# A pad of 384 bytes in the constants of an attention and expert kernel

## The chip, the cores and the metric

The kernel runs on one core of a Trainium2 chip. The metric is the time of one execution on the device in microseconds (us). The engines are TensorE (PE in the profile, with PEld for its weight loads), VectorE (DVE), ScalarE (ACT), GpSimd (POOL) and SyncE (SP); transfers run on 16 DMA engines.

## The reference

Linear attention with decay, and behind it a feed-forward pair of products with a SiLU. For 4 batches, 8 heads, 768 positions and head size 64, in blocks of 64 positions:

```
intra = (qb @ kb^T * Dmask) @ vb            # Dmask[i, j] = lam^(i-j) for i >= j, else 0
inter = (qb * lam^(pos+1)) @ kv_state
out   = intra + inter
kv_state = lam^64 * kv_state + (kb * lam^(63-pos))^T @ vb
```

The outputs of all heads, side by side, are x of 3072 tokens by 512. Then `h = x @ w_in` (512 by 2048), `g = h * sigmoid(h)`, `y = g @ w_out` (2048 by 512). All inputs and the output are float32; the kernel's products run in bfloat16.

## The kernel before

**Work.** The kernel takes the sequence in 12 pairs of 128-position units (two blocks of 128 to a pair, `U = 128`), 24 units in all. For each pair, `load_pair` (L358) issues the loads of k, q and v into staging tiles `raw` (4,096 bytes a partition; for pair 0 in two halves, tiles of 2,048 bytes). A DRAM run of one load is 512 bytes long: two positions of one head. `prepare` (L458) turns them into bfloat16: `cast` (L467) gives `kq`, `scale_v` (L470) gives `vd`, v times its decay. k and q are then turned head-dimension-first into `kqT`: for the first four pairs by PE (L510) and a copy, from the fifth on by a DMA transpose from `kq` to `kqT` (L525). Scores, states and outputs of the attention are small matmuls on quarters of the array (L558, L565, L591, L602 and, for the first pairs, L692, L772, L803, L811, L822); VectorE masks the scores into `st` with `tri` (L346 is the helper `mult`, L337 and L341 the helper `copy`), carries the state over `y` and `xf`, and writes the attention's output, scaled, into `xt`.

**Weights.** `load_w` (L377) loads w_in and w_out in 16 halves of 512 KB into the same staging tiles (`raw_w`; a DRAM run is 2,048 bytes), and each half is cast in two pieces by GpSimd, ScalarE or VectorE into `w_in_bf` and `w_out_bf` (L332 and L333, 16,384 bytes a partition each), which stay for the whole run.

**Products.** `product1` (L846) multiplies `w_in_bf` by `xt` (L858) and ScalarE takes the SiLU into `g` (L874); `product2` (L882) multiplies `g` by `w_out_bf` (L893), a copy brings the bank to `osb`, and ScalarE's queue stores it (L909). The last unit is stored in two halves of 128 KB.

**Order.** Nothing is scheduled at run time. `Planner` (L38) takes every piece of work with an estimated cost, and writes out one order for each engine (L932); the launch then issues the work in that order (L955 to L964). Loads stand in SyncE's queue in the order of `sequence` (L399), and the DMA transposes stand in the same queue; the stores have ScalarE's. In the first 19 us small matmuls on the tile `ones` (L930) are put into PE's planned gaps.

**Memory.** All constants come from one pool, `const`, and all working tiles from another, `sb`; a tile is placed behind the one allocated before it, at a multiple of 32 bytes. The order of the constants is `lam_sb`, `ones`, `ident`, `spot`, `row_i`, `tri`, `xe_all`, `xs_all`, `pose`, `row`, `log_all`, `log_lam`, `lam_v`, `lam_xe`, `lam_be`, `w_in_bf`, `w_out_bf`; behind them come the working tiles, in the order of their first use. `ones` is made at L291:

```
    ones = const.tile([128, 512], BF16, name="ones")
    nc.vector.memset(ones, 1.0)
    halves = [slice(0, 64), slice(64, 128)]
    ident = const.tile([128, 128], BF16, name="ident")
```

Of the kernel before, what the change touches and what calls it, by code (L numbers as in the profile page):

```python
# [8 lines left out]
F32 = mybir.dt.float32  # L9
# [222 lines left out]
def kernel(  # L232
# [30 lines left out]
    const = ctx.enter_context(tc.tile_pool(name="const", bufs=1))  # L263
# [27 lines left out]
    ones = const.tile([128, 512], BF16, name="ones")  # L291
    nc.vector.memset(ones, 1.0)  # L292
    halves = [slice(0, 64), slice(64, 128)]
    ident = const.tile([128, 128], BF16, name="ident")
    nc.gpsimd.memset(ident, 0.0)
    nc.gpsimd.affine_select(
# [698 lines left out]
```

## Time and profile before

| what | value |
|---|---|
| median of 3 runs | 215.47 us (215.08 to 215.98) |
| the profiled execution's own time | 215.7 us |
| its span, first to last instruction | 213.7 us |
| granted PE clock, mean | 0.998 |
| PE busy | 204.7 us, 2364 matmuls |
| ScalarE, VectorE, GpSimd busy | 115.5, 109.8, 22.6 us |
| moved by DMA | 38.09 MB in 62247 packets, mean 178 GB/s |
| of that SyncE's queue (q1) | 31.46 MB in 58480 packets |
| of that ScalarE's queue (q10) | 6.30 MB in 3744 packets |

The page shows one profiled execution. Its rows give busy time with its share of the span and, behind an x, the count of instructions; rows in slices cut the span into 40 equal parts, a digit being the busy share in tenths. The chain that ended last is followed back from the last instruction to what released each step. In the timeline a line is start, duration, engine, source line, operation, output <- input, shape and count, and in brackets the idle time before it with what ended it. A row of a DMA queue gives packets, MB and the packets' time as a share of 16 engines' time in the window asked for; packets overlap, so that share can pass 100%. A row of a stage gives its bounds and length, the busy time of PE, PEld, DVE, ACT and POOL with their counts, the granted clock, the DMA engines' share and GB/s.

### The profile page before, as it was taken

To read this page: it belongs to the slowest core of one execution; us is meant where nothing else is said; L and a number is where in the kernel's file an instruction comes from. 1 tells how busy PE (TensorE), PEld (TensorE's weight loads), DVE (VectorE), ACT (ScalarE), POOL (GpSimd) and SP (SyncE) were. 2 spreads that over 40 slices of the span, in tenths; PEclk is the share of its full clock that TensorE was granted. 3 is DMA by queue.
4 is the path that set the end of the run, shared out by engine and by line. 5 is a ranking of instruction groups with operands and counts; after the bars stand their busy time and mean duration, and the time that the engine had idled before them with its cause. 6 is when DMAs were issued, how large, how long until landed. Compare 5 with 4: busy or idle time off the path is not lost.

```text
span 213.7 us, 5445 instructions
## 1 busy us (share of the span) xinstructions
PE 204.7 (96%) x2364; PEld 122.5 (57%) x2364; DVE 109.8 (51%) x188; ACT 115.5 (54%) x169; POOL 22.6 (11%) x39
## 2 busy tenths in 40 slices
PE   7788989999899999999999999999999999999994
PEld 2666777776666557676765545454444444444453
DVE  3788849688523849688988696557011100111000
ACT  3665867758571686537596773514444444444121
POOL 4005421222100400001120010300000000000000
PEclk9999999999999999999999999999999999999999
DMA  4999999999999999899999251011011001110212
GB/s 119 294 324 363 351 326 278 377 287 377 213 326 290 296 284 319 156 248 295 241 277 222 66 101 49 5 52 49 0 52 49 13 36 49 49 52 0 98 49 98
DMA packets 62247, 38.09 MB, mean 178 GB/s; under 512 B 18064, under 2 KB 55184, under 8 KB 62224
## 3 DMA queue, kind: packets, MB, share of 16 engines
q1 hardware_dynamic: 58480, 31.46, 58.2%
q10 hardware_dynamic: 3744, 6.30, 8.0%
q8 instruction: 18, 0.29, 0.6%
q14 instruction: 5, 0.04, 0.1%
HBM read 27.27 MB, written 6.29 MB: 157 GB/s over the span
## 4 chain that ended last, share of the span: by engine, by line
PE 75%; DMA 12%; SPq 8%; DVE 2%; ACT 1%; issue 1%; POOL 1%
PE banks L893 37%; PE banks L858 31%; DMA raw_w<-in_moe_w_out_dram 7%; DMA raw<-in_q_dram 5%; SPq L364 4%; SPq L383 4%; PE banks L602 2%; PE banks L558 2%; PE banks L565 1%; DVE st L346 1%; PE banks L591 1%; POOL w_out_bf L343 1%; ACT g L874 0%; DVE kq L341 0%; PE banks L510 0%
## 5 line engine op out<-in xcount | busy, mean ns | idle before, releaser
L858 PE MATMUL banks<-xt,w_in_bf 128*128 128x256 bf16 (+1 forms) x576 | 116.1, 308 | 0.9 <-DVE st L346 0.7
L893 PE MATMUL banks<-w_out_bf,g 128*128 128x512 bf16 (+1 forms) x400 | 113.3, 371 | 0.7 <-POOL w_out_bf L343 0.7
L874 ACT ACTIVATE g<-banks 128x512 bf16<-128x512 f32 x96 | 70.1, 742 | 63.3 <-PE banks L858 57.1
L858 PEld LDWEIGHTS <-w_in_bf 128*128 128x128 bf16 x576 | 55.4, 98 | 31.6 <-POOL w_in_bf L343 1.2
L893 PEld LDWEIGHTS <-g 128*128 128x128 bf16 x400 | 38.5, 98 | 40.4 <-issue 1.2
L341 DVE COPY osb<-banks 128x512 f32<-128x512 f32 x13 | 9.0, 692 | 57.0 <-PE banks L893 51.7
L346 DVE TENSOR_TENSOR st<-banks,tri 128x512 bf16<-128x512 f32 (+1 forms) x42 | 29.6, 757 | 3.4 <-PE banks L602 2.4
L339 ACT ACTIVATE kq<-raw 64x512 bf16<-64x512 f32 (+2 forms) x32 | 24.0, 780 | 4.1 <-DMA raw<-in_k_dram 1.7
L346 DVE TENSOR_TENSOR xt<-banks,lam_xe 128x512 bf16<-128x512 f32 x24 | 15.7, 686 | 14.4 <-PE banks L558 13.6
L346 POOL TENSOR_TENSOR xf<-y,lam_be 128x256 f32<-128x256 f32 (+1 forms) x13 | 11.0, 848 | 89.3 <-DVE y L720 89.3
L341 DVE CAST kq<-raw 64x512 bf16<-64x512 f32 (+3 forms) x26 | 13.4, 534 | 5.6 <-DMA raw<-in_k_dram 2.7
L346 DVE TENSOR_TENSOR vd<-raw,lam_v 128x1024 bf16<-128x1024 f32 (+1 forms) x13 | 15.0, 1152 | 1.8 <-DMA raw<-in_v_dram 1.8
L339 ACT ACTIVATE osb<-banks 128x512 f32<-128x512 f32 (+1 forms) x12 | 6.7, 561 | 16.5 <-PE banks L893 16.5
L930 PE MATMUL banks<-ones 128*128 128x128 bf16 (+1 forms) x88 | 9.7, 259 | 1.5 <-DVE ones L292 1.5
L346 DVE TENSOR_TENSOR xs_all<-y,lam_be 64x256 bf16<-64x256 f32 (+2 forms) x21 | 10.4, 497 | 0.4
L602 PE MATMUL banks<-kqT 64*64 64x128 bf16 x288 | 9.5, 217 | 0.0
L930 PEld LDWEIGHTS <-ones 128*128 128x128 bf16 x88 | 5.9, 102 | 3.9 <-issue 2.1
L602 PEld LDWEIGHTS <-kqT 64*64 64x64 bf16 x288 | 7.4, 107 | 0.0
L510 PE MATMUL banks<-ident,kq 128*128 128x128 bf16 x64 | 5.3, 220 | 1.9 <-DVE kq L341 1.4
L720 DVE TENSOR_TENSOR y<-banks,xf 128x256 f32<-128x256 f32 (+1 forms) x17 | 6.7, 398 | 0.6 <-POOL xf L346 0.5
L591 PE MATMUL banks<-vd,kq 64*64 64x64 bf16 x240 | 6.9, 194 | 0.0
L339 ACT ACTIVATE kqT<-banks 128x512 bf16<-128x512 bf16 (+1 forms) x6 | 4.9, 810 | 2.7 <-PE banks L510 2.7
(50 smaller groups left out, 79.0 us busy)
## 6 DMA issues: line engine op xcount, KB each, us to landing
out_dram<-osb ACTq DMA_DIRECT2D x23, 256.0 KB, 2.0
raw<-in_k_dram SPq DMA_DIRECT2D x11, 512.0 KB, 6.6
raw<-in_q_dram SPq DMA_DIRECT2D x11, 512.0 KB, 7.1
raw<-in_v_dram SPq DMA_DIRECT2D x11, 512.0 KB, 7.5
raw_w<-in_moe_w_in_dram SPq DMA_DIRECT2D x8, 512.0 KB, 8.8
raw_w<-in_moe_w_out_dram SPq DMA_DIRECT2D x8, 512.0 KB, 7.0
raw<-in_k_dram SPq DMA_DIRECT2D x2, 256.0 KB, 5.2
raw<-in_q_dram SPq DMA_DIRECT2D x2, 256.0 KB, 5.6
```

The lines of the kernel that those rows point to most:

```text
L339: nc.scalar.activation(o, i, AF.Copy)
L341: nc.vector.tensor_copy(o, i)
L346: (nc.vector if e == "DVE" else nc.gpsimd).tensor_tensor(o, a, b, op=AL.mult)
L364: nc.sync.dma_start(out=tile_of(bufs[i, g], [128, 2 * len(ms), 128], F32, "raw"), in_=src[i][heads(ms)].rearrange("h (p r) d -> p h (r d)" ...
L383: nc.sync.dma_start(out=tile_of(b, [128, 2, 512], F32, "raw_w"), in_=w_in_r[:, 2 * h:2 * h + 2, cs] if what == "i" else w_out_r[:, 4 * j + ...
L591: mm = nc.tensor.matmul(psum_of(db)[d, 256 * c + 64 * k:256 * c + 64 * k + 64], lhsT=kq_of()[halves[c], 0, r, 2 * k + (h ^ c if n in CROSS ...
L602: nc.tensor.matmul(t[c, k % 2, r, :], lhsT=t_of()[halves[row], 0, r, k, c], rhs=t_of()[halves[row], 1, :, k, c], start=(k % 2 == 0 and r = ...
L720: nc.vector.tensor_tensor(tile_of(src, [128, NP, 64], F32, "y")[:, sl], d_of(), old[0].tile[:, sl], op=AL.add)
L858: nc.tensor.matmul(t[:, j, :], lhsT=w_in_bf[:, ko, 128 * m:128 * m + 128], rhs=xt[gi].tile[:, ko, :], start=(ko == 0), stop=(ko == KI - 1))
L874: nc.scalar.activation(t, psum_of(bank).rearrange("p (jc r a) -> p jc r a", r=2, a=64), AF.Silu)
L893: nc.tensor.matmul(psum_of(bank)[:, :w], lhsT=g.tile[:, j, 128 * gp:128 * gp + 128], rhs=w_out_bf[:, ko, cs], start=(ko == 0), stop=(ko == ...
L930: nc.tensor.matmul((t if b.pool == "bank" else t[:, 0])[:, 0:w], lhsT=ones[:, 0:128], rhs=ones[:, 0:w], start=True, stop=True)
```

## The change

One tile of 96 float32 elements, 384 bytes in each of the 128 partitions, is allocated from `const` between `ones` and `ident`. Nothing writes or reads it. Every tile that is allocated later lies 384 bytes higher.

```
     halves = [slice(0, 64), slice(64, 128)]
+
+    const.tile([128, 96], F32, name="pad")
     ident = const.tile([128, 128], BF16, name="ident")
```

## The prediction

> **What bounds the kernel now.** I read the page first: the shares by engine, the forty slices, then the chain that ended last. Two stretches show: in the first quarter the DMA engines are full and TensorE (PE) has gaps; behind it PE is the bound.
>
> ```profile
> span 213.7 us, 5445 instructions
> PE 204.7 (96%) x2364; PEld 122.5 (57%) x2364; DVE 109.8 (51%) x188; ACT 115.5 (54%) x169; POOL 22.6 (11%) x39
> ...
> DMA  4999999999999999899999251011011001110212
> ...
> PE 75%; DMA 12%; SPq 8%; DVE 2%; ACT 1%; issue 1%; POOL 1%
> ```
>
> A slice is 213.7 / 40 = 5.34 us. The DMA row is full to slice 21, about 112 us. Of the chain 75% is PE; the 12% DMA and 8% SPq (SyncE's queue, held up while it issues loads) are what a change to transfers can touch. Next I asked where in time that 20% lies: the chain in order of time, from 18 us to 60 us.
>
> ```profile
> 18.44 9.64 DMA raw<-in_q_dram
> ...
> 28.11 0.70 DVE kq L341
> ...
> 34.19 6.50 DMA raw_w<-in_moe_w_out_dram
> ...
> 40.74 0.88 POOL w_out_bf L343
> ...
> 46.83 8.54 DMA raw_w<-in_moe_w_out_dram
> ...
> 55.42 0.62 POOL w_out_bf L343
> ```
>
> All of it lies before 55.42 us. The last transfer on the chain is a half of w_out that lands at 46.83 + 8.54 = 55.37 us; GpSimd casts it, and PE goes on. Then I asked for busy time by stage (busy us of each engine, the granted clock, the DMA share, GB/s).
>
> ```profile
> 18.00:28.00 10.00, 9.06 (x140) 6.94 (x129) 7.25 (x14) 7.63 (x12) 4.89 (x8) 1.00 1.10 345
> 28.00:42.00 14.00, 13.25 (x191) 10.35 (x189) 10.37 (x14) 9.96 (x15) 2.72 (x4) 1.00 1.07 327
> 42.00:56.00 14.00, 13.55 (x182) 9.30 (x180) 10.60 (x20) 9.31 (x14) 3.31 (x5) 1.00 1.09 325
> 56.00:112.00 56.00, 55.92 (x789) 37.49 (x789) 38.36 (x65) 34.92 (x53) 5.70 (x6) 1.00 1.14 266
> 112.00:150.00 38.00, 37.84 (x513) 19.70 (x511) 26.59 (x47) 20.16 (x30) 2.49 (x3) 1.00 0.35 78
> ```
>
> PE lacks 0.94 us in 18 to 28, then 0.75 and 0.45 us, but 0.08 us in the 56 us behind that, although the DMA engines are as full there (share 1.14). A busy PE need not run at its peak, so one row of the whole chain checks it:
>
> ```profile
> 72.63 6.04 PE banks L893 x28
> ```
>
> 28 matmuls of 512 columns in 6.04 us are one each 0.216 us, 2.37 columns a nanosecond, at a granted clock of 1.00; the 0.376 to 0.39 us that a single one lasts is latency that overlaps. From 56 us PE streams without a break, and an earlier transfer is worth nothing there. So the change is worth what it takes out of PE's gaps before 56 us. These are PE's gaps after 18 us with what ended them, from the timeline, and beside the first one the two instructions that ended just before it:
>
> ```profile
> 19.56 1.37 PE L858 MATMUL banks<-xt,w_in_bf 128*128 128x256 bf16 x11 [0.74 <-DVE st L346]
> 28.86 0.62 PE L510 MATMUL banks<-ident,kq 128*128 128x128 bf16 x8 [0.59 <-DVE kq L341]
> 41.66 0.81 PE L893 MATMUL banks<-w_out_bf,g 128*128 128x512 bf16 x3 [0.16 <-POOL w_out_bf L343]
> 56.08 1.02 PE L893 MATMUL banks<-w_out_bf,g 128*128 128x512 bf16 x4 [0.54 <-POOL w_out_bf L343]
> ```
>
> ```profile
> 18.86 0.63 ACT L339 ACTIVATE w_in_bf<-raw_w 128x512 bf16<-128x512 f32 x1 [0.72 <-DMA raw_w<-in_moe_w_in_dram]
> 18.32 1.21 DVE L346 TENSOR_TENSOR st<-banks,tri 128x1024 bf16<-128x1024 f32 x1
> ```
>
> The first gap is put down to the mask on VectorE (DVE), which ended at 18.32 + 1.21 = 19.53. But the matmul reads xt and w_in_bf, not st, and a cast of w_in_bf that had waited for its transfer ended at 18.86 + 0.63 = 19.49: I take it for a DMA gap too. So all four gaps hang on transfers: 0.74 + 0.59 + 0.16 + 0.54 = 2.03 us.
>
> **The change part by part.** It adds no instruction, no wait and no DMA, and the planner's costs are not touched, so each engine's order should stay the same. It moves every tile allocated behind `ones` by 384 bytes. In the program before, `w_in_bf` begins at byte 27,776 of a partition, which is 54 x 512 + 128. `w_in_bf`, `w_out_bf` and all tiles behind them have sizes that are multiples of 1,024 bytes, so all of them begin 128 bytes past a multiple of 512, and after the change at one. Since 384 is 3 x 128, no address changes its place within a line of 128 bytes. Only what works in pieces of 256 or 512 bytes can tell the difference: I cost the engines' own reads and writes at nothing (PE above streams at full rate from the shifted tiles already), and look at the DMAs.
>
> What does a DMA packet cost? The first view is a stretch in which only q, k, v travel (pieces of 512 bytes), the second one with weights alone (2,048 bytes), the third the start, whose queue q10 carries the little load of lam (pieces of 32 bytes), the last everything up to 56 us.
>
> ```profile
> DMA packets 1160, 0.58 MB, mean 292 GB/s; under 512 B 18, under 2 KB 1160, under 8 KB 1160
> ```
>
> ```profile
> DMA packets 407, 0.78 MB, mean 391 GB/s; under 512 B 25, under 2 KB 25, under 8 KB 407
> ```
>
> ```profile
> q10 hardware_dynamic: 137, 0.00, 1.5%
> ```
>
> ```profile
> DMA packets 21981, 17.29 MB, mean 309 GB/s; under 512 B 729, under 2 KB 17877, under 8 KB 21973
> ```
>
> The first two stretches are 2 us long. Sixteen engines for 2,000 ns carry 1160 - 18 = 1142 pieces of 512 bytes: 28.0 ns each. In the second, 382 pieces of 2,048 bytes: 83.8 ns, less some 0.5 ns for the 25 small ones, 83.3 ns. The difference, 55.3 ns for 1,536 bytes, is 0.036 ns a byte, so a 512-byte piece is 18.4 ns of bytes and 9.6 ns fixed. A third of the time of a q, k or v load is a fixed price per packet; 391 GB/s in the second stretch against 292 in the first shows that the memory does not set the pace of the small ones. The lam load's packets cost 1.5% x 16 x 4,000 ns / 137 = 7.0 ns with 1.2 ns of bytes, so 5.8 ns fixed. These are too short to cross a 256-byte line, all others cross one or more and start off it. So 9.6 - 5.8 = 3.8 ns of a packet could be the price of the broken start.
>
> The trace has no load to an address on a 512-byte line, so the saving is bounded, not read: at most 9.6 ns a packet (all that is fixed), and nothing, or below nothing, at the other end. I take 3.8 ns, by the lam row, the nearest that lacks the broken start. Up to 56 us there are 21981 - 729 = 21252 packets, 1328 on each engine, so each nanosecond saved lands the last half of w_out 1.33 us earlier; 3.8 ns give 5.0 us. Does the saving come in time for each gap? The packets up to 18, 28 and 41 us:
>
> ```profile
> DMA packets 7227, 4.71 MB, mean 262 GB/s; under 512 B 329, under 2 KB 6473, under 8 KB 7226
> ```
>
> ```profile
> DMA packets 10985, 8.16 MB, mean 292 GB/s; under 512 B 430, under 2 KB 9211, under 8 KB 10983
> ```
>
> ```profile
> DMA packets 15793, 12.39 MB, mean 302 GB/s; under 512 B 558, under 2 KB 12847, under 8 KB 15789
> ```
>
> Less the small ones these are 6898, 10555 and 15235; by 16 and 3.8 ns, 1.6, 2.5 and 3.6 us. PE needs 0.74, 1.33 and 1.49 us there, and 2.03 at the end: covered each time, and a saving of 2.03 / 1.33 = 1.53 ns a packet already closes the last gap. So the size of the saving hardly matters, if there is one: **the gaps cap the gain at 2.03 us**. Next late is PE itself. The cap may leak both ways: VectorE is busy 7.25 of 10 us around the first gap and its mask ends 0.03 us before PE starts, so 0.74 may not come back whole; and the PE work before 18 us may begin a little earlier, since VectorE's scaling of v waits for a landing there:
>
> ```profile
> 16.15 1.44 DVE L346 TENSOR_TENSOR vd<-raw,lam_v 128x1024 bf16<-128x1024 f32 x1 [0.38 <-DMA raw<-in_v_dram]
> ```
>
> That is 0.38 us more at best. Behind 56 us, and in the stores, I cost the change at nothing: PE hides loads, transposes and stores, and only the last store is bare, with eight pieces of 1,024 bytes to an engine, 0.03 us at 3.8 ns.
>
> Sum: 215.7 us (the profiled execution, span 213.7 and 2.0 around it) - 2.03 = 213.7. Its time lies 0.23 above the median of 215.47, so against that: **213.4 us**.
>
> A rule of the Trainium skill bears on this. "DMA: Bandwidth & Descriptors", section "How a descriptor splits into AXI transactions", says that a transaction must start on a 256-byte line, and that a descriptor which does not fetches the bytes below its start as well and pays their beats. Here that would be 128 bytes, four beats; at the page's clock of 850 MHz some 4.7 ns, an estimate from it. It would give the same capped sum as my 3.8 ns. But it is worded for reads, and speaks against the change so far: the loads read device memory and only write the tiles. By the wording, only stores and transposes gain, which is the first rival's time.
>
> **The rivals.** *The loads don't care* (or the allocator drops a tile that nobody uses, and nothing moves). The fixed 9.6 ns may be the price of any large packet, and the 5.8 of a small one. For it: the stores, which read the tiles, cost about what the loads do,
>
> ```profile
> q10 hardware_dynamic: 1152, 2.10, 10.1%
> ```
>
> (150 to 205 us: 10.1% x 16 x 55,000 / 1152 = 77 ns on the mean of 2,048-byte pieces and one small in nine, some 86 ns for a large one), though reading and writing need not be hurt alike. Then only stores and transposes could gain, behind PE: 0.03 us at the last store, 215.4 us.
>
> *The loads become dearer.* One mechanism: pieces that all begin on a 512-byte line fall on the same part of the memory where they were spread before, and each packet waits one step more. For the price I take the same 3.8 ns, with the other sign: the last half of w_out lands 5.0 us later, PE has nothing to put in its place, 215.5 + 5.0 = 220.5 us. There is no cap on this side. It decides from 0.8 ns a packet (0.8 x 1.33 = 1.08 us, half a per cent). For it speaks nothing in the trace but that it cannot exclude it; against it, that it is the packets with broken starts whose fixed price is the larger.
>
> **How the numbers follow.** About 0.5%, 1.1 us, is what a measurement of this kernel can tell from no change. Forecast 213.4: 0.52, of which 0.03 falls within half a per cent (a saving under 0.8 ns). Loads don't care, 215.4: 0.34, with 0.02 on either side for what else shifts. Dearer, up to 220.5: 0.14. So faster 0.49 + 0.02 = 0.51, same 0.03 + 0.30 = 0.33, slower 0.14 + 0.02 = 0.16. The forecast's own range is 212.8 (the cap, 0.38 us before 18 us and the spread of the runs, 0.3) to 214.4; to hold 8 in 10 it must reach the first rival's 215.4 and its spread: 212.8 to 216.0. Left out are the dearer packets.
>
> **What would show it.** Right: the two 2 us stretches carry more than 1142 and 382 pieces; the casts of w_out wait less; the gap before PE at 56 us is gone; PE from there on takes as long as before. Wrong: the same 28.0 and 83.3 ns a packet (then the loads don't care), or the packets get cheaper and the gaps stay, held by VectorE's mask or a cast. Fewer packets in such a stretch, and a longer gap before the last cast of w_out, are the dearer loads.

## The result, and the profile after

The changed kernel takes 212.66 us (median of 6 runs, 212.10 to 214.22) against 215.98 us (median of 6, 215.08 to 216.35) for the kernel before: a ratio of 0.986, 95% interval 0.982 to 0.990. The profiled execution took 212.1 us, its span is 210.1 us, 3.6 us shorter than before; it is the fastest of the six, and between the medians lie 3.3 us. The order of the instructions on every engine is the same in both, so the two profiles can be laid on each other line by line; line numbers are higher by 2.

The page of the changed kernel: span, busy time, the slices of the DMA engines, SyncE's queue, and the chain that ended last.

```profile
span 210.1 us, 5445 instructions
...
PE 203.6 (97%) x2364; PEld 122.4 (58%) x2364; DVE 109.4 (52%) x188; ACT 115.1 (55%) x169; POOL 23.6 (11%) x39
...
DMA  4999999999999997999974141011011101110212
...
q1 hardware_dynamic: 58480, 31.46, 52.7%
...
PE 93%; DMA 2%; POOL 1%; DVE 1%; issue 0%; SPq 0%; ACT 0%; POOLq 0%; DVEq 0%
```

The same 58480 packets move the same 31.46 MB, but take 52.7% of 210.1 us where they took 58.2% of 213.7: 124.4 and 110.7 us of packet time on each of 16 engines. The chain has turned: PE from 75% to 93%, DMA from 12% to 2%, and SyncE's queue from 8% to nothing. Now the stages (the same columns as before: busy us of PE, PEld, DVE, ACT, POOL, granted clock, DMA share, GB/s).

```profile
18.00:28.00 10.00, 9.91 (x144) 7.96 (x143) 7.25 (x13) 8.43 (x13) 4.76 (x7) 1.00 1.10 373
28.00:42.00 14.00, 14.00 (x246) 10.60 (x244) 10.97 (x16) 10.05 (x15) 2.46 (x4) 1.00 1.07 340
42.00:56.00 14.00, 14.00 (x136) 10.24 (x135) 10.97 (x22) 9.65 (x14) 2.92 (x4) 1.00 1.12 328
56.00:112.00 56.00, 56.00 (x785) 36.86 (x783) 39.19 (x66) 34.79 (x52) 5.67 (x5) 1.00 1.03 273
```

PE's gaps of 0.94, 0.75 and 0.45 us are 0.09, 0 and 0. The timeline of PE shows how far each step has come forward: these are the matmuls that began at 18.20, 28.86 and 56.08 us before.

```profile
17.21 2.04 PE L860 MATMUL banks<-xt,w_in_bf 128*128 128x256 bf16 x15 [0.43 <-POOL w_in_bf L345]
...
26.43 0.62 PE L512 MATMUL banks<-ident,kq 128*128 128x128 bf16 x8
...
52.52 1.03 PE L895 MATMUL banks<-w_out_bf,g 128*128 128x512 bf16 x4
```

0.99 us at the first product, 2.43 at the second mark, 3.56 at the third, and 3.6 at the end of the span. Everything is won before 56 us, and nothing is lost or won behind it. Between the first two marks lie 0.69 us at the next product (19.56 before, 17.88 now, in the middle of the first row) and 0.74 at the transposes; between the last two 0.32 at the products of w_out that began at 41.66, 0.13 at one that began at 52.46, and 0.70.

Last the packets, in the 2 us of the changed kernel that the prediction used for the 512-byte pieces, and in 2 us that hold weights alone:

```profile
DMA packets 1363, 0.70 MB, mean 352 GB/s; under 512 B 21, under 2 KB 1361, under 8 KB 1362
```

```profile
DMA packets 414, 0.80 MB, mean 400 GB/s; under 512 B 23, under 2 KB 23, under 8 KB 414
```

1340 pieces of 512 bytes where there were 1142, so at most 23.9 ns each for 28.0; and 391 pieces of 2,048 bytes where there were 382. The short pieces have become 4 ns cheaper; the long ones have hardly changed.

### The profile page after: what moved, and what is told of

Its sections match the earlier page's. It is cut to its first block, busy times and chain, and to the rows that moved or that the text cites. A ratio compares the mean times of both kernels' runs of the same rounds, so it can differ in the third digit from the quotient of the medians.

```text
span 210.1 us, 5445 instructions
## 1 busy us (share of the span) xinstructions
PE 203.6 (97%) x2364; PEld 122.4 (58%) x2364; DVE 109.4 (52%) x188; ACT 115.1 (55%) x169; POOL 23.6 (11%) x39
## 3 DMA queue, kind: packets, MB, share of 16 engines
q1 hardware_dynamic: 58480, 31.46, 52.7%
## 4 chain that ended last, share of the span: by engine, by line
PE 93%; DMA 2%; POOL 1%; DVE 1%; issue 0%; SPq 0%; ACT 0%; POOLq 0%; DVEq 0%
PE banks L860 40%; PE banks L895 40%; PE banks L560 2%; DMA raw<-in_v_dram 2%; PE banks L604 2%; PE banks L512 2%; PE banks L567 1%; PE banks L932 1%; PE banks L593 1%; PE banks L824 1%; POOL xf L348 1%; PE banks L774 1%; POOL w_in_bf L345 1%; SPq L366 0%; PE banks L805 0%
## 5 line engine op out<-in xcount | busy, mean ns | idle before, releaser
L860 PEld LDWEIGHTS <-w_in_bf 128*128 128x128 bf16 x576 | 55.4, 98 | 31.3 <-POOL w_in_bf L345 0.9
L348 POOL TENSOR_TENSOR xf<-y,lam_be 128x256 f32<-128x256 f32 (+1 forms) x13 | 12.0, 926 | 89.4 <-DVE y L722 89.4
L348 DVE TENSOR_TENSOR vd<-raw,lam_v 128x1024 bf16<-128x1024 f32 (+1 forms) x13 | 14.7, 1134 | 1.3 <-DMA raw<-in_v_dram 1.3
L593 PEld LDWEIGHTS <-kq 64*64 64x64 bf16 x240 | 5.7, 109 | 0.9 <-issue 0.7
```

Of the source, the lines that this page charges most:

```text
L348: (nc.vector if e == "DVE" else nc.gpsimd).tensor_tensor(o, a, b, op=AL.mult)
L593: mm = nc.tensor.matmul(psum_of(db)[d, 256 * c + 64 * k:256 * c + 64 * k + 64], lhsT=kq_of()[halves[c], 0, r, 2 * k + (h ^ c if n in CROSS ...
L860: nc.tensor.matmul(t[:, j, :], lhsT=w_in_bf[:, ko, 128 * m:128 * m + 128], rhs=xt[gi].tile[:, ko, :], start=(ko == 0), stop=(ko == KI - 1))
```

## The experiments

My theory after the result: a short piece that begins off a 256-byte line in the staging tile is dearer by some 4 ns, and that alone makes the gain. Rivals: the line is one of 512 bytes; the price goes by the bytes below the start, as the rule of the Trainium skill has it ("DMA: Bandwidth & Descriptors", section "How a descriptor splits into AXI transactions"); or the loads have no part in it, and the other tiles gain. Ratios are to the kernel before, run on the same chip. Code is shown in part and against the changed kernel; the remarks behind # are not in the kernels.

**Loads alone.** A kernel that only loads, 4 MB at a time, into one tile at various distances from a 512-byte line, and then stores. All products, casts and masks are left out.

```
PHASES = [(512, 0), (512, 128), (2048, 0), (2048, 128), (512, 256), (512, 32), (512, 64), (512, 384), (2048, 256),
          (512, 0), (512, 128)]
...
        for i in range(8):
            o = off // 4 + 1024 * i
            to = buf[:, o:o + 1024]
```

> All products, casts and masks are left out; the outputs are rows of the loaded tile. SyncE alone loads 11 times 4 MB into one tile, with nothing beside it: pieces of 512 bytes that begin 0, 128, 256, 32, 64, 384, 0 and 128 bytes past a 512-byte line, and pieces of 2,048 bytes at 0, 128 and 256; then 12 stores of 256 KB read the tile at 128 and 12 at 0. Before: 28.0 ns a 512-byte piece and engine, 83.3 ns a 2,048-byte one. Lines of 256 bytes: 512-byte pieces take some 24 ns at 0 and 256 and some 28 ns at 32, 64, 128 and 384. Lines of 512 bytes: 24 ns at 0 alone, 28 at 256 too. Bytes below the start (the rule's beats): 24 at 0 and 256, about 25 at 32, 26 at 64, 28 at 128 and 384. Contention with the engines' reads, not the pieces themselves: the same at every offset. For the 2,048-byte pieces, a price per packet would give some 79 ns at 0 and 256 against 83 at 128.

Packets in 2 us of this kernel, once a phase runs evenly: 512-byte pieces at 0, at 128, at 256 and at 32 bytes past the line.

```profile
DMA packets 1382, 0.69 MB, mean 347 GB/s; under 512 B 26, under 2 KB 1382, under 8 KB 1382
```

```profile
DMA packets 1150, 0.58 MB, mean 290 GB/s; under 512 B 16, under 2 KB 1150, under 8 KB 1150
```

```profile
DMA packets 1371, 0.69 MB, mean 347 GB/s; under 512 B 16, under 2 KB 1371, under 8 KB 1371
```

```profile
DMA packets 1145, 0.58 MB, mean 289 GB/s; under 512 B 16, under 2 KB 1145, under 8 KB 1145
```

Without the small ones, 32,000 ns hold 1356, 1134, 1355 and 1129 pieces: 23.6 ns on a line of 256 bytes, 28.2 to 28.3 off it. The phases at 64 and 384 bytes (1134 and 1135 pieces) and the repeats of 0 and 128 say the same. So it is the line of 256 bytes, not of 512; and 32 bytes off cost what 128 do. That last point is not the rule's: a beat for each 32 bytes below the start would have made the piece at 32 bytes some 25 ns, an estimate by the clock of that page of the Trainium skill. The engines' reads have no part, since no engine read the tile in these windows.

**Other sizes, and stores.** The same kernel with pieces of 256 to 2,048 bytes, each on the line and 128 bytes off it, and the stores apart from the loads.

```
PHASES = [(512, 0), (512, 128), (256, 0), (256, 128), (1024, 0), (1024, 128), (1536, 0), (1536, 128), (2048, 0), (2048, 128)]
```

> All products, casts and masks are left out; the outputs are rows of the loaded tile. As loads_alone, with other piece sizes, each first on a 512-byte line and then 128 bytes off: 512, 256 (half the bytes), 1,024, 1,536 (three quarters), 2,048 from w_out; then 12 stores off the line and 12 on it, apart from the loads. In loads_alone a 512-byte piece took 28.2 ns off the line and 23.6 on it. A fixed price of a broken start, 4.7 ns a piece at every size: 256 some 14 against 19 ns, 1,024 some 42 against 47, 1,536 some 61 against 66, 2,048 some 80 against 85. A price that only shows where a piece is short, hidden behind something else in long ones: the difference is there at 256 and 512 and shrinks to nothing by 2,048, as the two phases of loads_alone look. Stores, which read the tile: 4.7 ns dearer off the line if the rule's beats hold, the same if not.

Four of its 2 us views: 1,024 bytes on the line and off it, 1,536 on it and off it.

```profile
DMA packets 770, 0.77 MB, mean 385 GB/s; under 512 B 18, under 2 KB 770, under 8 KB 770
```

```profile
DMA packets 697, 0.70 MB, mean 349 GB/s; under 512 B 16, under 2 KB 697, under 8 KB 697
```

```profile
DMA packets 540, 0.79 MB, mean 394 GB/s; under 512 B 31, under 2 KB 539, under 8 KB 539
```

```profile
DMA packets 546, 0.79 MB, mean 395 GB/s; under 512 B 32, under 2 KB 546, under 8 KB 546
```

| piece | on the line, ns | off it, ns |
|---|---|---|
| 256 bytes | 14.8 | 18.8 |
| 512 | 23.6 | 28.2 |
| 1,024 | 42.6 | 47.0 |
| 1,536 | 63.0 | 62.3 |
| 2,048 (loads_alone) | 81.0 | 81.4 |

Each is 32,000 ns by the pieces in the best even 2 us of its phase. A short piece pays 4.0 to 4.6 ns for a start off the line, whatever its length up to 1,024 bytes; from 1,536 bytes on a load pays nothing that can be seen. These long phases do not run evenly (windows of 2 us from 88 to 62 ns at 1,536), so a small price could hide there; 4.6 ns would show in the best windows, which differ by less than 1 ns. The stores read the tile in pieces of 2,048 bytes: first off the line, then on it.

```profile
DMA packets 415, 0.76 MB, mean 381 GB/s; under 512 B 43, under 2 KB 43, under 8 KB 415
```

```profile
DMA packets 445, 0.81 MB, mean 404 GB/s; under 512 B 51, under 2 KB 51, under 8 KB 445
```

372 against 394 pieces: some 86 and 81 ns, so on the reading side a long piece does pay about 5 ns. In the attention kernel the stores are hidden and this is worth nothing. Why a long write is spared stays open.

**Pad of 128 bytes.** All tiles behind the constants at 256 past a multiple of 512.

```
-    const.tile([128, 96], F32, name="pad")
+    const.tile([128, 32], F32, name="pad")
```

> Pad of 128 bytes in place of 384: weights and all tiles behind them begin 256 bytes past a multiple of 512. If lines of 256 bytes decide, the time is that of the changed kernel, ratio 0.986 to before, some 212.7 us. If lines of 512 bytes decide, each 512-byte piece still crosses one, and it is that of before, 1.00, or between.

212.42 us, ratio 0.986 (0.984 to 0.989): the whole gain. A line of 256 bytes is enough.

**Pad of 416 bytes.** All tiles 32 bytes past a multiple of 512.

```
-    const.tile([128, 96], F32, name="pad")
+    const.tile([128, 104], F32, name="pad")
```

> Pad of 416 bytes: weights and all tiles behind them begin 32 bytes past a multiple of 512, so every 512-byte piece crosses a line of 256 and one of 512, but lies only 32 bytes off. If crossing decides, ratio 1.00 to before, 215 to 216 us. If the bytes below the start decide (one beat in place of four), a quarter of the price stays: ratio 0.988 to 0.99, some 213 us, near the changed kernel.

216.01 us, ratio 1.002 (1.000 to 1.004): the whole gain is lost. That a piece begins off the line decides, not how far off.

**Staging tiles alone on the line, and its reverse.** The staging tiles get a pool of their own; a small tile in front of one pool puts the other working tiles, or in the reverse the staging tiles, 128 bytes off.

```
+    stage = ctx.enter_context(tc.tile_pool(name="stage", bufs=1))
+    sb.tile([128, 32], F32, tag="off", name="off")        # stage_only
+    stage.tile([128, 32], F32, tag="off", name="off")     # stage_off, with
+    sb.tile([128, 96], F32, tag="on", name="on")
+            where = stage if b.pool in ("raw", "rawh") else sb
```

> The staging tiles raw lie in a pool of their own on multiples of 512 bytes, weights too; all other working tiles (kq, kqT, vd, st, xt, xf, y, g, osb) lie 128 bytes off, as before. If the loads into the staging tiles are what gains, the time is that of the changed kernel, ratio 0.986, some 212.7 us. If it is the engines' reads and writes of the other tiles, or the DMA transposes and stores, it is that of before, 1.00.

> The reverse of stage_only: the staging tiles raw begin 128 bytes off the line, weights and all other working tiles on it. If the loads into the staging tiles are the whole of it, ratio 1.00 to before, 215 to 216 us; if the other tiles have a share, below that by the share.

Staging alone on the line: 212.62 us, ratio 0.987 (0.984 to 0.990). Staging alone off it: 215.65 us, 1.000 (0.998 to 1.002). The loads of q, k, v and the weights into these tiles are the whole of the gain; no run here moved the two kinds apart, and that the weights' loads have little part in it follows from the prices by length above. The weights' place, the transposes, the stores and what the engines read and write have none that can be measured. In the reverse, PE's gaps are back where they were, here the one at 28.86 us and the one behind it:

```profile
28.86 0.62 PE L516 MATMUL banks<-ident,kq 128*128 128x128 bf16 x8 [0.59 <-DVE kq L347]
41.53 0.81 PE L899 MATMUL banks<-w_out_bf,g 128*128 128x512 bf16 x3 [0.24 <-POOL w_out_bf L349]
```

**The first pair off the line.** Everything on the line but the six staging tiles of pair 0.

```
+    head = ctx.enter_context(tc.tile_pool(name="head", bufs=1))
+    head.tile([128, 32], F32, tag="off", name="off")
+    sb.tile([128, 96], F32, tag="on", name="on")
+            where = head if b.pool == "rawh" else sb
```

> Everything on the line but the six staging tiles of pair 0, which lie 128 bytes off: 3072 pieces, 192 on each engine, at 4.7 ns 0.9 us. The prediction gave the stretch before 18 us 0.38 us at best; the changed kernel's first product of w_in started 0.99 us earlier. If the start counts in full, this kernel's first product comes some 0.7 to 0.9 us later than the changed kernel's and the end with it: ratio 0.990 to before, some 213.4 us. If the start is worth what the prediction said, or the later gaps take it up, 0.986 to 0.988, 212.7 to 213 us.

212.98 us, ratio 0.988 (0.986 to 0.991): at the upper end of the second expectation, and not told apart from the changed kernel. Its profile has the first product at 17.38 us and the next at 18.25:

```profile
17.38 0.61 PE L864 MATMUL banks<-xt,w_in_bf 128*128 128x256 bf16 x4 [0.31 <-POOL w_in_bf L349]
18.25 1.38 PE L864 MATMUL banks<-xt,w_in_bf 128*128 128x256 bf16 x11 [0.26 <-POOL w_in_bf L349]
```

0.17 and 0.37 us behind the changed kernel, far less than 0.9. But stage_only, whose first pair is on the line, has its second one at 18.21 too. So pair 0 by itself is worth little; how the 0.99 us of the start divide over the later loads I did not settle.

**Fewer fillers.** 44 fewer matmuls on `ones`.

```
-                    occupy(b, int((start - at) / 0.056 * 0.75), 128)
+                    occupy(b, int((start - at) / 0.056 * 0.35), 128)
```

> The changed kernel with 44 fewer matmuls on ones in PE's planned gaps of the first 19 us (factor 0.35 in place of 0.75). With the loads earlier, the fillers, sized for the old pace, stand ahead of real work: in the changed kernel the 22 at 9.06 us run to 10.4 us, half a us behind the copy of kqT that the next matmuls need. If PE's order is what now limits the start, the first product of w_in comes up to 0.5 us earlier and the end with it, ratio 0.984. If VectorE and GpSimd limit it, nothing, 0.986. If PE's clock drops for want of work, slower than the changed kernel.

212.87 us, ratio 0.988 (0.985 to 0.991): no difference. In place of the fillers PE waits longer for the cast of w_in, 0.81 us where it was 0.43:

```profile
17.34 0.61 PE L860 MATMUL banks<-xt,w_in_bf 128*128 128x256 bf16 x4 [0.81 <-POOL w_in_bf L345]
```

**The wait that took the place of the others.** In the changed kernel PE waits 0.43 us at 17.21 us for GpSimd's cast. GpSimd's timeline there, the changed kernel and then the kernel before:

```profile
14.74 1.77 POOL L348 TENSOR_TENSOR xf<-y,lam_be 128x128 f32<-128x128 f32 x2 [11.58 <-DVE y L722]
16.45 1.37 POOL L345 CAST w_in_bf<-raw_w 128x512 bf16<-128x512 f32 x2
```

```profile
15.76 0.76 POOL L346 TENSOR_TENSOR xf<-y,lam_be 128x128 f32<-128x128 f32 x2 [12.59 <-DVE y L720]
17.54 0.61 POOL L343 CAST w_in_bf<-raw_w 128x512 bf16<-128x512 f32 x1 [1.02 <-DMA raw_w<-in_moe_w_in_dram]
```

The two products that took 0.76 us take 1.77, since v has landed and VectorE scales it (14.67 to 15.88) at the same time; before, GpSimd's products began first and VectorE's scaling took 1.44 us in place of 1.21. The Trainium skill has this rule ("SBUF — State Buffer", section "Who interferes with whom": a VectorE instruction with both inputs in SBUF shuts out a GpSimd one that reads it, and the one that starts first keeps the port), and both orders here agree with it. Behind that the cast starts late, although ScalarE finds its half landed at 15.90. Two variants, beside the changed kernel on the same chip:

```
-    HOME = {('cast', 3, 0, 1): 'ACT', ('cast w', 1, 3): 'POOL'}
+    HOME = {('cast', 3, 0, 1): 'ACT', ('cast w', 1, 3): 'POOL', ('xf', 0, 0, 1): 'DVE', ('xf', 0, 1, 1): 'DVE'}    # xf_on_vector
```

```
-WIDE, CAST, LARGE, PLAIN, TURN = (512, 24.0, 27.0), (256, 14.0, 31.0), (2048, 92.0, 92.0), (2048, 84.0, 84.0), (1024, 46.0, 46.0)
+WIDE, CAST, LARGE, PLAIN, TURN = (512, 20.0, 23.6), (256, 14.0, 31.0), (2048, 92.0, 92.0), (2048, 84.0, 84.0), (1024, 46.0, 46.0)    # planned_for_pace
```

> The changed kernel as it is, on the same chip as the two variants beside it, so that these can be compared with it: ratio to before 0.986, 212 to 213 us.

> The changed kernel, with the two xf products of pair 0 given to VectorE in the plan. In the changed kernel they run on GpSimd at 14.74 us, beside VectorE's scaling of v, and take 1.77 us in place of 0.76; the cast of w_in behind them starts at 16.45 although its half has landed by 15.90, and PE waits 0.43 us for it at 17.21. If that is the next thing on the path, the first product of w_in comes 0.3 to 0.4 us earlier and the end with it: 0.998 of the changed kernel. If VectorE's own queue, two products longer, is late in its place, or the next half of w_in is, no difference.

> The changed kernel, with the planner told the new price of a 512-byte piece (20.0 and 23.6 ns in place of 24.0 and 27.0), so that order and fillers suit the earlier landings. If the old order holds the changed kernel back, 0.3 to 0.8 us faster than it, ratio to before some 0.983. If the order was right for either pace, no difference; a planner that counts on data too early could put a wait into PE, 0.5 us slower.

The changed kernel again: 212.67 us, ratio 0.988 (0.985 to 0.992). With xf on VectorE: 214.52 us, 0.995 (0.993 to 0.998). Planned for the new pace: 214.97 us, 0.998 (0.996 to 1.001). Both lose most of the gain, more than either expectation allowed. The first does what it was meant to: the cast starts at 16.03 us and the first product at 16.70, half a us earlier. But the planner lays out everything behind it anew, and PE then meets a wait on VectorE that was not there. PE's timeline of xf_on_vector:

```profile
16.70 0.28 PE L860 MATMUL banks<-xt,w_in_bf 128*128 128x256 bf16 x1 [0.53 <-POOL w_in_bf L345]
...
26.45 0.92 PE L860 MATMUL banks<-xt,w_in_bf 128*128 128x256 bf16 x7 [1.22 <-DVE xt L348]
```

So the 0.43 us is a real wait, but neither variant pays. In planned_for_pace PE waits for casts of w_out again, 0.62 us at 48.37 and 0.56 at 53.53; which part of the new order costs most, in either variant, was not tested. Such waits also differ between two executions of one kernel: the profile of the changed kernel run again (213.28 us) has one that the profile above lacks.

```profile
39.57 0.81 PE L895 MATMUL banks<-w_out_bf,g 128*128 128x512 bf16 x3 [0.71 <-POOL w_out_bf L345]
```

No version was clearly faster than the changed kernel.

## Where the prediction was right and where it was off

- **Where the bound lies: right.** All of the gain came ahead of 56 us, and PE's time behind that did not move: 3.56 us ahead at that mark, 3.6 at the end.
- **The price of a packet: the size right by chance, its make-up wrong.** I took 3.8 ns for every packet, from the packets of lam. Pieces of 512 bytes give 4.6 ns, the weights' pieces of 2,048 next to nothing. Of some 1328 packets an engine up to 56 us, 256 are weights (16 halves of 512 KB are 4096 pieces on 16 engines); the other 1072 at 4.6 ns make 4.9 us, where I had 5.0. The split into "bytes" and "fixed", from one short and one long size, mixed two kinds: the short pieces had the broken start in them and the long ones did not, so both terms came out wrong. And lam's 7.0 ns is how long a packet was recorded, while 28.0 and 83.3 ns are the pace at which overlapping packets follow each other (recorded, a packet of the first stretch takes 113.6% x 32,000 / 1160 = 31.3 ns); that the difference came near 4.6 is luck.
- **The cap by the gaps: the term that was too small.** I summed 0.74 + 0.59 + 0.16 + 0.54 = 2.03 us of idle time. The same four steps gave 0.69 + 0.74 + 0.32 + 0.70 = 2.45. The idle time in brackets counts from the modelled end of the matmul before; but that matmul, of 0.273 us (256 columns) or 0.379 us (512), makes way for the next after 0.108 or 0.216 us when there is one, by the row of 28 matmuls in 6.04 us. So each bracket leaves out 0.165 us: 2.03 + 0.66 = 2.69. Most of the 0.24 that is missing to that is a rest of the first gap: the matmul at 17.88 begins 0.33 us after the one before it, in place of 0.11, and GpSimd's second cast, in the row at 16.45 above, ends at 17.82. It has no bracket in the timeline, and shows only in the starts of single matmuls. I had read the row of 28 matmuls, and used it for PE's rate alone.
- **The start before 18 us: not in the sum, and the largest miss.** I allowed 0.38 us at best, from VectorE's wait for v. It gave 0.99. The loads were on the path there too. PE's own timeline before says so, but my list of gaps began at 18 us:

```profile
8.11 0.32 PE L692 MATMUL banks<-vd,kq 64*64 64x64 bf16 x16 [0.34 <-DVE vd L346]
9.52 0.40 PE L510 MATMUL banks<-ident,kq 128*128 128x128 bf16 x4 [0.20 <-DVE kq L341]
12.77 0.62 PE L510 MATMUL banks<-ident,kq 128*128 128x128 bf16 x8 [0.37 <-ACT kq L339]
```

After the change the first is 0.20 us and the other two are gone. What stands behind the third is ScalarE's cast of k of pair 1, before and then changed,

```profile
11.65 1.06 ACT L339 ACTIVATE kq<-raw 128x1024 bf16<-128x1024 f32 x1 [1.10 <-DMA raw<-in_k_dram]
```

```profile
10.64 1.06 ACT L341 ACTIVATE kq<-raw 128x1024 bf16<-128x1024 f32 x1 [0.78 <-DMA raw<-in_k_dram]
```

which waited 1.10 us for its transfer; PE's transposes of pair 1 come behind it, at 12.77 us before and 11.75 now. Fillers hid part of the waiting: in the changed kernel with 44 fewer of them PE has gaps of 0.54, 0.51, 0.39 and 0.35 us between 7 and 16 us. The last work ahead of the first product, before and then changed,

```profile
17.64 0.45 PE L692 MATMUL banks<-vd,kq 64*64 64x64 bf16 x32
```

```profile
16.35 0.42 PE L694 MATMUL banks<-vd,kq 64*64 64x64 bf16 x32
```

is 1.29 us earlier, and the new wait at 17.21 takes 0.3 us of that back. So 0.99 + 2.45 + 0.13 = 3.57 us in place of 2.03, in the profiled executions; between the medians of 215.98 and 212.66 us it is 3.3. The time came out 0.7 us below the 213.4 forecast, just under the range's low end of 212.8.

- **What is late next: half right.** VectorE's mask was not it; GpSimd's cast was, through the products beside VectorE's scaling.
- **The rule of the Trainium skill.** The estimate of 4.7 ns for 128 bytes is what a short piece pays (4.6), and on the reading side the stores' 5 ns agree with it. But the price of a load is the same at 32 bytes, and it falls on writes, of which the wording does not speak. That the loads gain settles the first rival; that the kernel with staging tiles off the line is no slower than before, and that on the line each piece is cheaper, settles the second: nothing became dearer.

## What to carry to other kernels

Put tiles that DMAs fill in short pieces at multiples of 256 bytes: the allocator packs at 32, and a few small constants in front can put every tile behind them off the line. It pays where loads of 1,024 bytes or less to a row set the pace; look for PE gaps that end in a cast behind a transfer. When summing such gaps, add to each the part of the last matmul's recorded time in which the next one could already have run, and do not take an engine that runs fillers for one that is not waiting.

## What the runs showed of the hardware

- A load's write that starts off a 256-byte line costs 4.0 to 4.6 ns more a piece at 256, 512 and 1,024 bytes, the same from 32 to 384 bytes past the 512-byte line, and nothing that could be seen at 1,536 and 2,048 bytes; a store's read in pieces of 2,048 bytes costs about 5 ns more.
- The price does not show at once. In loads_alone the phase at 384 bytes past the line is issued from 118.67 us on; its windows of 2 us from 122 us and from 128 us (packets, then the queue's row):

```profile
DMA packets 1193, 0.60 MB, mean 300 GB/s; under 512 B 23, under 2 KB 1193, under 8 KB 1193
## 3 DMA queue, kind: packets, MB, share of 16 engines
q1 hardware_dynamic: 1193, 0.60, 119.3%
```

```profile
DMA packets 1151, 0.58 MB, mean 291 GB/s; under 512 B 16, under 2 KB 1151, under 8 KB 1151
## 3 DMA queue, kind: packets, MB, share of 16 engines
q1 hardware_dynamic: 1151, 0.58, 119.8%
```

Without the packets under 512 bytes, 1170 pieces land in the first and 1135 in the second, while the summed packet time stays the same share of 16 engines' 2 us. So a packet is recorded as longer: 119.3% x 32,000 / 1193 = 32.0 ns, then 119.8% x 32,000 / 1151 = 33.3 ns. The change is sharp: from 120.9 to 122.4 us the phase moves 345 GB/s, the pace of pieces on the line, and from there to 124 us 289 GB/s; the other phases of 512-byte pieces off the line start alike. It looks as if a buffer had filled up; that is an inference, and no run tested it.
